# Attention scores of a head pair: one 128-row matmul with zero-padded queries, or two 64-row matmuls in the row halves of TensorE

## The chip, the cores and the metric

The kernel runs on one core of one Trainium2 chip. The metric is device time in microseconds (us) of one execution. Names used below: PE is TensorE's matmul stream, PEld its weight loads, DVE is VectorE, ACT is ScalarE, SP is the engine that issues many of the loads. A "profile" is one execution recorded by the hardware profiler; a "timed run" has only its time.

## The reference, cut to what matters

Attention over 8 batches of 8 heads with a window of 128 positions comes first. Its output goes through a mixture of 8 experts whose routing weights are normalised over all tokens.

```python
# q, k, v: (8, 8, 576, 64)
scores = scale * np.matmul(q, k.transpose(0, 1, 3, 2))
# ... bias by distance, mask (0 <= rel < 128), softmax
x = np.matmul(attn, v)                  # -> (4608, 512)
P = np.exp(x @ w_gate - max)            # ... eight rounds of row and column normalisation
for e in range(8):
    out += P[:, e:e+1] * (np.maximum(x @ w1[e], 0.0) @ w2[e])
```

## The kernel before

The head size is 64; the matmuls use up to 128 rows of TensorE (the trace lists them as 128*128, rows by columns). The kernel keeps two heads in one 128-row tile: head A in rows 0 to 63, head B in rows 64 to 127. To get two separate scores from one 128-row matmul, the queries are stored twice as wide, with zeros in the rows of the other head: `QZ[0:64, j, 0]` holds head A, `QZ[64:128, j, 1]` holds head B, the other two quarters are zero. The zeros are written once, at the start.

```python
KTs = [asb.tile([P, NPR, S], FP16, name=f"KT{i}") for i in range(2)]
QZs = [asb.tile([P, NPR, 2, S], FP16, name=f"QZ{i}") for i in range(2)]
...
def tr_unit(b, nm, j):                       # turns keys or queries of one head pair
    psT = aps.tile([P, RT, RP], FP16, ..., tag="pmm", bufs=4)
    ...                                      # 8 transposes on TensorE
    if nm == "k":
        nc.scalar.copy(out=KTs[b % 2][:, j, :]..., in_=psT...)
    else:
        QZ = QZs[b % 2]
        nc.vector.tensor_copy(
            out=QZ[0:64, j, 0, :].rearrange("p (c r i) -> p r c i", r=RT, i=HI),
            in_=psT[0:64].rearrange("p r (c i) -> p r c i", i=HI))
        nc.vector.tensor_copy(
            out=QZ[64:128, j, 1, :].rearrange("p (c r i) -> p r c i", r=RT, i=HI),
            in_=psT[64:128].rearrange("p r (c i) -> p r c i", i=HI))

def scores(b, kb, half):                     # key block kb, four heads; 80 calls in all
    ...                                      # nk keys (128 or 64), nq queries (256, 192 or 64)
    ps = aps.tile([P, 2, 2, 2 * P], FP32, ..., tag="psS")        # one buffer
    for jj in range(2):
        nc.tensor.matmul(
            out=ps[0:nk, jj, :, 0:nq],
            lhsT=KT[:, 2 * half + jj, k0 : k0 + nk],
            rhs=QZ[:, 2 * half + jj, :, k0 : k0 + nq])
    pt = asb.tile([P, 4, 2 * P], FP16, ..., tag=f"pt{half}", bufs=3)
    nc.scalar.activation(
        out=pt[0:nk, :, 0:nq],
        in_=ps[0:nk].rearrange("p a b q -> p (a b) q")[:, :, 0:nq],
        func=AF.Exp, scale=scale)
    ...
```

The output of attention is a matmul per head with 65 columns (`psN`). Its transposed copy (`psXT`), the turned keys and queries (`psT`), the routing scores (`psG`) and the two layers of expert 0 (`psh`, `psy`) share **one pool of four PSUM buffers**, the tag "pmm". So a matmul into the pool can be held up by whichever engine still reads the buffer that it is given (in the profile before, 0.38 us by ScalarE at 103.92 us, below):

```python
psT  = aps.tile([P, RT, RP], FP16, ..., tag="pmm", bufs=4)   # queries: read by VectorE
psXT = aps.tile([P, NDT, P], FP16, ..., tag="pmm", bufs=4)   # read by VectorE
psG  = aps.tile([P, E],     FP32, ..., tag="pmm", bufs=4)   # read by ScalarE
psh, psy: tag "pmm" too, 4                                   # read by ScalarE
```

Keys and queries of batch b + 2 are loaded while batch b is worked on. Expert 0 is interleaved with attention, so PE has something to do from about 50 us on. After attention the other experts run as a sequence of tasks; for each, the input block (`xl`) and a broadcast row of routing weights (`Pb`) are loaded three tasks ahead, and VectorE multiplies them before PE can use the result:

```python
def load_p(j):
    Pbs[j] = msb.tile([P, GT], FP32, name=f"Pb_{e}_{g}", tag="Pb", bufs=2)
    nc.sync.dma_start(out=Pbs[j], in_=PTr[e : e + 1, GT * g : ...].to_broadcast([P, GT]))

def load_next(h):
    if h + 3 < NT:
        load_x(h + 3, tasks[h + 3][1])
        load_p(h + 3)
```

The softmax here doesn't subtract the row's maximum and nothing guards it: scores larger than these inputs give would overflow.

## Time and profile before

| quantity | value | view |
|---|---|---|
| time, median of the first 6 runs | 1045.55 us (1045.15 to 1046.12) | timed runs |
| span of the profiled run | 1042.3 us | head of the page |
| attention ends (last routing-score matmuls) | 210.8 us | timeline |
| PE busy, 50 to 200 us | about 24 of each 25 us | table by stretches |
| VectorE busy there | about 18 of each 25 us | table by stretches |

The first lines of the page give busy time, share of the span and count of instructions:

```profile
PE 1004.1 (96%) x9163; PEld 817.6 (78%) x9163; DVE 841.7 (81%) x1318; ACT 647.9 (62%) x1176; POOL 233.6 (22%) x242
```

The table by stretches, of the kernel before. Columns: the stretch, then busy us and count of PE, PEld, DVE, ACT and POOL, as the first line has them.

```profile
core 0: us, PE busy (x) PEld busy (x) DVE busy (x) ACT busy (x) POOL busy (x), PEclk, DMA share, GB/s
...
50.00:75.00 25.00, 24.32 (x269) 14.38 (x266) 18.05 (x40) 17.59 (x30) 7.48 (x9) 1.00 0.83 97
```

PE is nearly full and VectorE has a quarter of its time free.

The timeline at 19 us, of the kernel before. Columns: start, length, engine, line, operation, output<-inputs, sizes, count, and in brackets the idle time before it and what ended it.

```profile
19.24 1.01 PE L237 MATMUL psS_1_0_228<-QZ_78,KT_76 128*128 128x512 f16 x2 [1.11 <-ACT pt_0_1_225 L245]
...
21.36 1.01 PE L237 MATMUL psS_1_1_234<-QZ_78,KT_76 128*128 128x512 f16 x2 [1.11 <-ACT pt_1_0_231 L245]
```

Here PE is not full: a half-block takes 21.36 - 19.24 = 2.12 us, of which PE idles 1.11 us until the exp has read the only scores buffer. And this is where the early stage ends, in the same view:

```profile
41.01 0.69 DVE L195 COPY kp_0_500<-kf_0_387 72x2048 f16<-72x2048 f16 x1
...
44.57 0.39 PE L325 MATMUL psXT_4_548<-ident,xsb_4_508 64*128 64x64 f16 x4
```

VectorE reorders the keys of batch 2 at 41.0 us, just after they have landed.

Last, what a change of the tile shape costs, at the end of attention in the same view. "128*128" is rows*columns of the array that the matmul uses.

```profile
205.84 0.29 PE L285 MATMUL psN_3_3124<-vsb_81,pt_3_0_3038 128*128 128x65 f16 x4
205.97 0.29 PE L285 MATMUL psN_3_3124<-vsb_81,pt_2_1_3001 128*128 128x65 f16 x4
...
207.41 0.32 PE L285 MATMUL psN_4_3146<-vsb_81,pt_3_0_3038 128*64 128x65 f16 x4 [1.02 <-DVE xsb_3_3123 L294]
207.65 0.31 PE L285 MATMUL psN_4_3146<-vsb_81,pt_4_0_3093 64*64 64x65 f16 x4
207.89 0.31 PE L285 MATMUL psN_4_3146<-vsb_81,pt_3_1_3066 128*64 128x65 f16 x4
```

Groups of four equal matmuls of one shape (`psN_3`) start 0.13 us apart. When the shape alternates between 128*64 and 64*64 (`psN_4`), they start 0.24 us apart.

### The profile page before, as it was taken

To read this page: it belongs to the slowest core of one execution; us is meant where nothing else is said; L and a number is where in the kernel's file an instruction comes from. 1 tells how busy PE (TensorE), PEld (TensorE's weight loads), DVE (VectorE), ACT (ScalarE), POOL (GpSimd) and SP (SyncE) were. 2 spreads that over 40 slices of the span, in tenths; PEclk is the share of its full clock that TensorE was granted. 3 is DMA by queue.
4 is the path that set the end of the run, shared out by engine and by line. 5 is a ranking of instruction groups with operands and counts; after the bars stand their busy time and mean duration, and the time that the engine had idled before them with its cause. 6 is when DMAs were issued, how large, how long until landed. Compare 5 with 4: busy or idle time off the path is not lost. (4 is left out here: it accounts for less than half of the span.)

```text
span 1042.3 us, 22521 instructions
## 1 busy us (share of the span) xinstructions
PE 1004.1 (96%) x9163; PEld 817.6 (78%) x9163; DVE 841.7 (81%) x1318; ACT 647.9 (62%) x1176; POOL 233.6 (22%) x242
## 2 busy tenths in 40 slices
PE   4999999999999999999999999999999999999996
PEld 2555555545888878888888888888888888888885
DVE  5777777576899988787788998888889988888875
ACT  3567666646899865665566656665665566655660
POOL 6332331020233321111112211111112112222234
PEclk9999999989999999999999999999999999999998
DMA  9977786184697795444436963444446646655546
GB/s 168 178 95 93 97 94 92 42 177 104 139 201 160 159 184 112 100 112 93 92 92 132 180 135 93 108 107 106 96 93 135 129 92 150 143 134 132 132 102 132
DMA packets 129609, 128.10 MB, mean 123 GB/s; under 512 B 49729, under 2 KB 107233, under 8 KB 129505
## 3 DMA queue, kind: packets, MB, share of 16 engines
q0 software_dynamic: 97376, 60.61, 43.6%
q1 hardware_dynamic: 31840, 65.79, 20.4%
q8 instruction: 71, 1.16, 0.4%
q14 instruction: 34, 0.27, 0.1%
q10 hardware_dynamic: 288, 0.26, 0.1%
HBM read 113.62 MB, written 16.66 MB: 125 GB/s over the span
## 5 line engine op out<-in xcount | busy, mean ns | idle before, releaser
L124 PEld LDWEIGHTS <-w1t_104 128*128 128x128 f16 x288 | 26.5, 100 | 29.2 <-issue 5.0
L654 PEld LDWEIGHTS <-w1t_3237 128*128 128x128 f16 x288 | 28.2, 98 | 5.2 <-issue 1.8
L654 PEld LDWEIGHTS <-w1t_3219 128*128 128x128 f16 x288 | 28.2, 98 | 4.8 <-issue 0.4
L654 PEld LDWEIGHTS <-w1t_8011 128*128 128x128 f16 x288 | 28.1, 98 | 4.4 <-issue 0.3
L654 PEld LDWEIGHTS <-w1t_7840 128*128 128x128 f16 x288 | 28.2, 98 | 4.0 <-issue 0.8
L654 PEld LDWEIGHTS <-w1t_5174 128*128 128x128 f16 x288 | 28.1, 98 | 3.8 <-issue 0.3
L654 PEld LDWEIGHTS <-w1t_10776 128*128 128x128 f16 x288 | 28.2, 98 | 3.6 <-issue 0.3
L654 PEld LDWEIGHTS <-w1t_3979 128*128 128x128 f16 x256 | 25.1, 98 | 2.9
L76 POOL DMA_DIRECT2D out_dram<-acc_lo x24 | 24.5, 1828 | 0.0
L184 POOL DMA_DIRECT2D vsb_81<-in_v_dram x20 | 17.8, 892 | 26.0 <-PE psN_4_905 L285 5.3
L184 POOL DMA_DIRECT2D vsb_80<-in_v_dram x20 | 18.3, 932 | 18.9 <-PE psN_4_1307 L285 5.7
L237 PEld LDWEIGHTS <-KT_76 128*128 128x128 f16 (+1 forms) x80 | 7.3, 106 | 13.1 <-issue 9.3
L506 POOL PARTITION_ALL_REDUCE ca_sb<-cs_sb x8 | 3.2, 396 | 64.0 <-DVE cs_sb L503 64.0
L310 PEld LDWEIGHTS <-xT 128*128 128x128 f16 x144 | 8.3, 100 | 8.4 <-DVE xT L334 1.6
L546 ACT ACTIVATE acc_lo<-acc_lo,Pe_sb 128x512 f32<-128x512 f32 (+1 forms) x24 | 14.8, 616 | 0.0
L237 PEld LDWEIGHTS <-KT_77 128*128 128x128 f16 (+1 forms) x80 | 7.1, 104 | 9.8 <-issue 5.5
L76 POOL DMA_DIRECT2D out_dram<-acc_hi x12 | 11.2, 2129 | 6.0 <-DVE acc_hi L770 6.0
L778 POOL DMA_DIRECT2D acc_lo<-st_1_0_3821 x1 | 1.2, 1242 | 36.3 <-ACT st_1_0_3821 L777 36.3
L654 PEld LDWEIGHTS <-ws_1_3535 128*128 128x128 f16 x72 | 6.9, 97 | 1.7 <-DVE xd_0_3543 L615 0.6
L654 PEld LDWEIGHTS <-ws_2_4301 128*128 128x128 f16 x72 | 7.0, 98 | 1.5 <-issue 0.7
L206 PE MATMUL psT_k_0_128<-ident,kp_0_124 72*128 72x72 f16 x8 | 0.7, 252 | 7.7 <-DVE kp_0_124 L195 7.7
L804 DVE TENSOR_TENSOR acc_lo<-acc_lo 128x512 f32<-128x512 f32 x12 | 7.7, 684 | 0.0
(4203 smaller groups left out, 3609.4 us busy)
## 6 DMA issues: line engine op xcount, KB each, us to landing
xTd<-xT SPq DMA_DIRECT2D x9, 512.0 KB
out_dram<-acc_lo SPq DMA_DIRECT2D x24, 128.0 KB
vsb_80<-in_v_dram POOLq DMA_DIRECT2D x16, 128.0 KB, 8.0
vsb_81<-in_v_dram POOLq DMA_DIRECT2D x16, 128.0 KB, 5.0
out_dram<-acc_lo SPq DMA_DIRECT2D x24, 64.0 KB
out_dram<-acc_lo POOLq DMA_DIRECT2D x24, 64.0 KB, 7.2
w1t_104<-in_moe_w_dram POOLq DMA_DIRECT2D x2, 512.0 KB, 10.4
w2t_117<-in_moe_w_dram POOLq DMA_DIRECT2D x1, 1024.0 KB, 15.1
```

The source lines that it names most:

```text
L76: eng.dma_start(out=out[t0 : t0 + HB, c0:c1].rearrange("(i r) d -> r i d", r=RT), in_=t[HB * c : HB * c + HB], **kw,)
L124: nc.tensor.matmul(out=psh, lhsT=w1t[:, dt, P * ft : P * ft + P], rhs=x[:, dt, :], start=(dt == 0), stop=(dt == NDT - 1),)
L184: nc.gpsimd.dma_start(out=vsb[0:nk, kb, :, 0:Dh], in_=v[b, :, k0 : k0 + nk, :].rearrange("h s d -> s h d"),)
L206: nc.tensor.matmul(out=psT[:, r, :], lhsT=tt[:, r, 2 * Dh * jj : 2 * Dh * jj + 2 * Dh], rhs=ident[0:RP, 0:RP], is_transpose=True, start=(r ...
L237: nc.tensor.matmul(out=ps[0:nk, jj, :, 0:nq], lhsT=KT[:, 2 * half + jj, k0 : k0 + nk], rhs=QZ[:, 2 * half + jj, :, k0 : k0 + nq],)
L310: nc.tensor.matmul(out=psG, lhsT=xT[:, dt, P * blk : P * blk + P], rhs=wg_sb[:, dt, :], start=(dt == 0), stop=(dt == NDT - 1),)
L506: nc.gpsimd.partition_all_reduce(ca_sb, cs_sb, P, bass_isa.ReduceOp.add)
L546: nc.scalar.mul(acc(blk)[:, c], acc(blk)[:, c], Pe_sb[:, 0, blk : blk + 1])
L654: nc.tensor.matmul(out=ps[:, f, :], lhsT=a[:, kt, f0 : f0 + P], rhs=b[:, kt, :], start=(m in (1, 5) and f == 0 and kt == 0), stop=(kt == 1 ...
L778: nc.gpsimd.dma_start(out=quad(self.g, rh, ch), in_=st, accum_op=ALU.add)
L804: tt(out=t, in0=t, in1=quad(g, 1, 1), op=ALU.add)
```

## The change

The intent: let each head of the pair use its own 64 rows of TensorE. The two row halves are to run at the same time, so that the two heads take the time of one, and no zeros are streamed. The queries need no padding, so each head pair is copied from PSUM by one VectorE instruction in place of two, and four memsets go. The layout of the scores in PSUM is swapped (head within the pair first), so that each row half writes its own half of the scores buffer, and the exp puts the order back.

```diff
-        QZs = [asb.tile([P, NPR, 2, S], FP16, name=f"QZ{i}") for i in range(2)]
+        QTs = [asb.tile([P, NPR, S], FP16, name=f"QT{i}") for i in range(2)]
@@ tr_unit
-                QZ = QZs[b % 2]
                 nc.vector.tensor_copy(
-                    out=QZ[0:64, j, 0, :].rearrange("p (c r i) -> p r c i", r=RT, i=HI),
-                    in_=psT[0:64].rearrange("p r (c i) -> p r c i", i=HI),
-                )
-                nc.vector.tensor_copy(
-                    out=QZ[64:128, j, 1, :].rearrange("p (c r i) -> p r c i", r=RT, i=HI),
-                    in_=psT[64:128].rearrange("p r (c i) -> p r c i", i=HI),
+                    out=QTs[b % 2][:, j, :].rearrange("p (c r i) -> p r c i", r=RT, i=HI),
+                    in_=psT.rearrange("p r (c i) -> p r c i", i=HI),
                 )
@@ scores
             for jj in range(2):
-                nc.tensor.matmul(
-                    out=ps[0:nk, jj, :, 0:nq],
-                    lhsT=KT[:, 2 * half + jj, k0 : k0 + nk],
-                    rhs=QZ[:, 2 * half + jj, :, k0 : k0 + nq],
-                )
+                for hh in range(2):
+                    rows = slice(Dh * hh, Dh * hh + Dh)
+                    nc.tensor.matmul(
+                        out=ps[0:nk, hh, jj, 0:nq],
+                        lhsT=KT[rows, 2 * half + jj, k0 : k0 + nk],
+                        rhs=QT[rows, 2 * half + jj, k0 : k0 + nq],
+                    )
...
-                out=pt[0:nk, :, 0:nq],
-                in_=ps[0:nk].rearrange("p a b q -> p (a b) q")[:, :, 0:nq],
+                out=pt[0:nk].rearrange("p (jj hh) q -> p hh jj q", hh=2)[:, :, :, 0:nq],
+                in_=ps[0:nk, :, :, 0:nq],
@@ start
-            for QZ in QZs:
-                nc.vector.memset(QZ[64:128, :, 0, :], 0.0)
-                nc.vector.memset(QZ[0:64, :, 1, :], 0.0)
```

More of the change, by code (lines that the diff above doesn't have):

```diff
@@ L233, in scores @@
             nq = min(2 * P, S - k0)
-            KT, QZ = KTs[b % 2], QZs[b % 2]
+            KT, QT = KTs[b % 2], QTs[b % 2]
             ps = aps.tile([P, 2, 2, 2 * P], FP32, name=f"psS_{b}_{kb}_{half}", tag="psS")
             for jj in range(2):
-                nc.tensor.matmul(
-                    out=ps[0:nk, jj, :, 0:nq],
-                    lhsT=KT[:, 2 * half + jj, k0 : k0 + nk],
-                    rhs=QZ[:, 2 * half + jj, :, k0 : k0 + nq],
-                )
+                for hh in range(2):
[5 more added lines that the diff above has]
+                    )
             pt = asb.tile(
```

## The prediction

> **What bounds the kernel now.** The change touches only attention, 0 to 211 us of 1042. In the table by stretches TensorE (PE) is busy about 24.2 of each 25 us from 50 to 200 us (VectorE 18, ScalarE 17), and PE's waits between 60 and 190 us sum to 5 us: the length of the PE stream binds. From 17 to 30 us the timeline shows another limit: half-block period 2.12 us, exp 1.02 us, then 1.1 us until the next scores are there (one scores buffer; granted clock half until 49 us). At 41.0 us VectorE reorders the keys of batch 2 just as they land (11.0 us after issue).
>
> **Removed.** Scores take 430 ns per call at full clock in key blocks 0-2 (two 512-column matmuls), 324 in block 3, 112 in block 4. Two concurrent 64-row matmuls halve that: 48 x 213 + 16 x 161 + 16 x 50 ns = 13.6 us at most. VectorE loses one of two 0.45 us query copies 32 times (14 us, but it has slack) and four 1.02 us memsets, which end before the first load lands: worth nothing.
>
> **Added.** 160 matmuls, and changes of PE's tile shape. [...]block 4 already uses 64-row and 64-column tiles, there starts are 121-124 ns apart where 32-33 is usual, 309 instead of 215 after a 512-column matmul; the next gap is 20-24 ns longer too. I take 94 + 24 ns going in, 94 + 10 coming out. In program order the shape changes 87 times in attention before, 201 after: 114 more.[...]
>
> A call at full clock then costs 94 + 24 + [...]214 + 104 = 463 ns against 430 (blocks 0-2), about 412 against 324 (block 3), some 26 ns less in block 4, where the switches exist. Some switches coincide with existing ones. Estimate for 50-205 us: 1.3 us lost[...].
>
> **Gained early.** First scores 0.5-1 us sooner (one query copy per pair); then 0.35 us per half-block while the chain exp, scores, exp rules at half clock[...]: 3 us by 30 us. The load landing at 40-41 us takes back part. I keep 2 us at 45 us. After attention everything only shifts.
>
> **Prediction.** 1045.55 - 2 + 1.3 = about 1045 us; 8 in 10 between 1041.5 and 1049.5. Faster by over 2%: 0.015; within: 0.95; slower by over 2%: 0.035.
>
> **What would show each step.**
> - [...]the second pair 107 ns after the first.
> - First start after a change of shape 94 ns later than the stream needs.
> - Half-block period at 19-28 us 1.75 instead of 2.12 us.
> - VectorE waiting for batch 2's keys near 40 us.
> - Last gate matmul within 3 us of 210.8 us.
> - VectorE busy 18 us less, the span unmoved by it.
>
> **What would make it wrong.** Row halves that do not overlap[...]; [...]the clock rising one step earlier or later than 49 us (its changes lie multiples of 3.4 us apart in this trace: 1.7 us either way), or falling again within attention.

Cut out of the text above is a term in the price of a call, for a later start of the second row half. With it the sum came to 463 ns; the terms that are left, 94 + 24 + 214 + 104, make 436 ns. The prices for blocks 3 and 4 seem to hold that term too, and the 1.3 us lost was worked out with it. A change of shape costs time; the price itself, 94 ns, is read from starts in the trace before (310 ns in place of 215 to the scores of block 4 at 109.48 us, 95 more).

Two of its statements, with their figures. That two 64-row matmuls run at once was an assumption; the trace after shows starts 3 ns apart at full clock. For the clock: in the trace before, 512-column matmuls start 427 ns apart up to 47.5 us and 215 ns apart from 48.3 us on. The recorded granted clock is 1.00 from 48.21 us, where its record begins (the views print 1.00 before that too, for want of a record), 0.50 from 208.63 and 1.00 again from 215.46 to 1034.66 us: stretches of 160.43, 6.83 and 819.20 us, or 47, 2 and 240 times 3.41 us. "Half clock" and "full clock" below mean these two.

## The result, and the profile after

| | before | after |
|---|---|---|
| median of all runs of the comparison | 1045.55 us (20 runs, 1042.37 to 1047.67) | 1044.61 us (10 runs, 1041.09 to 1046.48) |
| ratio | 1 | 0.9989, 95% interval 0.9978 to 1.0000 |
| profiled run | 1044.11 us, span 1042.3 | 1046.57 us, span 1044.7 |

Ratios here are the mean time of one kernel's runs over the mean of the other's of the same rounds, so they are not quite the ratio of the medians quoted. The verdict is "same": about 1 us faster. The profiled run of the kernel after was slower than all its timed runs, so the two spans stand the other way round; single profiles of one kernel here scatter by some 2 us. For that reason both kernels were profiled a second time (rep_before and rep_after below), and what is read from the profiles is read from stages, not from the span.

The page after, first lines and the lines by stretch and on the timeline that answer to those above:

```profile
PE 998.8 (96%) x9323; PEld 811.2 (78%) x9323; DVE 821.2 (79%) x1282; ACT 647.5 (62%) x1176; POOL 233.5 (22%) x242
```

```profile
50.00:75.00 25.00, 24.57 (x294) 13.95 (x291) 16.46 (x37) 17.97 (x32) 7.49 (x9) 1.00 0.90 102
```

```profile
18.83 0.61 PE L234 MATMUL psS_1_0_224<-QT_78,KT_76 64*128 64x256 f16 x4 [1.11 <-ACT pt_0_1_221 L242]
...
20.55 0.61 PE L234 MATMUL psS_1_1_232<-QT_78,KT_76 64*128 64x256 f16 x4 [1.11 <-ACT pt_1_0_229 L242]
...
42.89 0.69 DVE L195 COPY kp_0_510<-kf_0_393 72x2048 f16<-72x2048 f16 x1 [4.81 <-DMA kf_0_393<-in_k_dram]
...
45.07 0.39 PE L322 MATMUL psXT_4_562<-ident,xsb_4_520 64*128 64x64 f16 x4 [4.20 <-DVE xsb_4_520 L291]
```

Three readings. VectorE is busy 841.7 - 821.2 = 20.5 us less. A half-block of the early stage takes 20.55 - 18.83 = 1.72 us where it took 2.12. And at 42.9 us VectorE has waited 4.81 us for the keys of batch 2, where it had work before: whatever was gained by then is waited away, and the next matmuls start 0.50 us later than before (45.07 against 44.57). The load was issued at 29.67 us, 0.29 us sooner than before, and took 13.2 us where it had taken 11.0 (13.9 against 10.2 in the second pair); why it took longer is not shown.

Now the whole span, cut at four marks of the timeline: the second `psh` group of expert 0 (attention interleaved with expert 0 from there on), the last `psy` of it (`psy_23`), and the last routing-score matmuls, with which attention ends.

| stage, us | before | rep_before | after | rep_after |
|---|---|---|---|---|
| start to the second psh group | 48.30 | 48.05 | 48.63 | 48.18 |
| from there to psy_23 | 155.35 | 155.70 | 151.66 | 152.24 |
| to the last routing scores | 7.22 | 7.23 | 7.18 | 7.18 |
| all after attention | 831.43 | 833.62 | 837.24 | 838.03 |
| span | 1042.3 | 1044.6 | 1044.7 | 1045.6 |

So the middle of attention is 3.5 to 3.7 us shorter, in both pairs, and the part after attention, which the change does not touch, is 4.4 to 5.8 us longer. The lines at the end of attention, before and then after:

```profile
210.77 0.27 PE L310 MATMUL psG_3191<-wg_sb,xT 128*128 128x8 f16 x4 [0.39 <-DVE xT L334]
```

```profile
207.36 0.27 PE L307 MATMUL psG_3315<-wg_sb,xT 128*128 128x8 f16 x4 [0.39 <-DVE xT L331]
```

**The middle of attention: what PE's stream gained.** This is one scores call after, at full clock (granted clock 1.00 from 48.6 to 205.5 us), from the timeline, with the one before it on PE:

```profile
98.40 1.03 PE L124 MATMUL psh_2_0_1484<-xT,w1t_100 128*128 128x512 f16 x4
...
99.37 0.39 PE L234 MATMUL psS_2_1_1493<-QT_79,KT_77 64*128 64x256 f16 x4
...
99.69 0.30 PE L282 MATMUL psN_1_1501<-vsb_81,pt_0_0_1316 128*128 128x65 f16 x4
...
101.07 0.42 PE L206 MATMUL psT_q_1_1528<-ident,qp_0_1372 72*128 72x72 f16 x8
...
101.86 0.45 DVE L220 COPY QT_78<-psT_q_1_1528 128x576 f16<-128x576 f16 x1
...
102.36 0.59 PE L124 MATMUL psh_2_2_1569<-xT,w1t_100 128*128 128x512 f16 x2
```

and the same work before:

```profile
100.39 0.59 PE L237 MATMUL psS_2_1_1444<-QZ_79,KT_77 128*128 128x512 f16 x2
...
100.83 0.29 PE L285 MATMUL psN_1_1450<-vsb_81,pt_0_0_1274 128*128 128x65 f16 x4
...
102.20 0.42 PE L206 MATMUL psT_q_1_1477<-ident,qp_0_1328 72*128 72x72 f16 x8
...
102.98 0.44 DVE L221 COPY QZ_78<-psT_q_1_1477 64x576 f16<-64x576 f16 x1
...
103.44 0.46 DVE L225 COPY QZ_78<-psT_q_1_1477 64x576 f16<-64x576 f16 x1
103.69 0.17 ACT L317 ACTIVATE P_sb<-psG_1495 128x8 f32<-128x8 f32 x1
...
103.92 0.59 PE L124 MATMUL psh_2_2_1517<-xT,w1t_104 128*128 128x512 f16 x2 [0.38 <-ACT P_sb L317]
```

Matmuls with 512 columns start 0.215 us apart here, so the four of `psh_2_0` after have streamed by 98.40 + 0.86 = 99.26; the scores start at 99.37, some 0.1 us late, and the next group starts at 99.69. The call has cost 99.69 - 99.26 = 0.43 us (0.420 us by the unrounded starts). Before, it cost 100.83 - 100.39 = 0.44 us (0.432 us unrounded). The two halves together stream in half the time (by estimate twice 107 ns, half of the 215 ns of a 512-column matmul, in place of twice 215), and the two changes of shape take it back. The single starts in the trace show it: 96 ns beyond the stream going into the scores, then 3, 116, 3 ns between the four matmuls, and 202 ns from the last one to the next group, that is its 107 ns and 95 more.

Over the whole stretch I summed PE's start-to-start gaps. "Scores" is what the scores take, with what they add to the gap in front of them and behind them; "other waits" is all that the other gaps have beyond the streaming time.

| stretch from the second psh group to psy_23, us | before | after |
|---|---|---|
| scores with their changes of shape | 30.04 | 28.17 |
| other changes of shape | 3.44 | 3.42 |
| other waits | 5.95 | 4.16 |

Half of the gain is the scores (1.87 us), the other half is waits that have nothing to do with scores (1.79 us). The lines at 102 to 104 us show one of them: `psh_2_2` waits for a buffer of the shared pool. Before, two readers end shortly before it starts at 103.92: the second query copy (103.44 + 0.46 = 103.90), which reads `psT_q_1`, and ScalarE's `P_sb` (103.69 + 0.17 = 103.86), which reads `psG`. The bracket names `P_sb`, and pe_only, an experiment below that keeps both copies, shows that this is right. The same place there:

```profile
101.53 0.46 DVE L225 COPY QZ<-psT_q 64x576 f16<-64x576 f16 x1
...
101.73 0.17 ACT L319 ACTIVATE P_sb<-psG 128x8 f32<-128x8 f32 x1
...
101.95 1.02 PE L124 MATMUL psh<-xT,w1t 128*128 128x512 f16 x4 [0.28 <-ACT P_sb L319]
```

The matmul starts at 101.95, before the second copy ends at 101.99, and 0.05 us after `P_sb` ends, as in the kernel before. After, with one copy that ends at 101.86 + 0.45 = 102.31, `psh_2_2` starts at 102.36, with no idle time listed, and before `P_sb` begins (102.52). So it no longer waits for the same buffer. The programs agree: `psh_2_2` is given the buffer of `psG` in before and pe_only, and that of `psT_q_1` in after and dve_only. The second copy thus costs time at one remove: while it reads, the buffer of `psT_q_1` is not free (until 103.90), and the buffer given in its place is not free sooner. Waits of about 0.55 us stand six times in the profile before; five are for `P_sb`, one is for the second query copy itself. After, three of 0.44 us are left, all for `P_sb`, and the others are 0.07 us or less.

**After attention.** The view of waits of PE from 215 us on. Columns: engine, tile and line that waited, what it waited for, us in total, times, longest. Before:

```profile
PE lb_0_1_5245 L654 <- DVE lc_0_1_5270 L693: 1.3, 1, 1.3
PE lb_0_1_8271 L654 <- DVE lc_0_1_8301 L693: 0.6, 1, 0.6
```

and after:

```profile
PE lb_1_1_5624 L648 <- DVE lc_1_1_5655 L687: 1.5, 1, 1.5
PE lb_0_1_5369 L648 <- DVE lc_0_1_5394 L687: 1.4, 1, 1.4
PE lb_0_1_8395 L648 <- DVE lc_0_1_8425 L687: 1.3, 1, 1.3
PE lb_7_1_5023 L648 <- DVE lc_7_1_5052 L687: 1.0, 1, 1.0
```

All idle times of PE over 0.05 us from 215 us on sum to 3.46 us before (5.28 in rep_before) and 7.44 us after (8.64 in rep_after); the expectations below quote an earlier count, which is 0.1 to 0.4 us higher. VectorE itself was late at those places because a routing-weight row had not landed. One pair, on the timeline, before:

```profile
335.58 0.43 SPq L590 DMA_DIRECT2D Pb_8_4801<-PTd  x1
...
342.02 1.22 DVE L597 TENSOR_TENSOR xl_4799<-xl_4799,Pb_8_4801 128x1024 f16<-128x1024 f16 x1
...
387.03 1.22 DVE L597 TENSOR_TENSOR xl_5406<-xl_5406,Pb_1_5408 128x1024 f16<-128x1024 f16 x1
```

and after:

```profile
333.25 0.53 SPq L584 DMA_DIRECT2D Pb_8_4925<-PTd  x1
...
340.85 1.23 DVE L591 TENSOR_TENSOR xl_4923<-xl_4923,Pb_8_4925 128x1024 f16<-128x1024 f16 x1 [1.06 <-DMA Pb_8_4925<-PTd]
...
387.69 1.23 DVE L591 TENSOR_TENSOR xl_5530<-xl_5530,Pb_1_5532 128x1024 f16<-128x1024 f16 x1 [1.78 <-DMA Pb_1_5532<-PTd]
```

The load has about 6.5 us from issue to use, with nothing to spare: before, it was just enough here, after, it was 1.06 us too late, and 1.78 us too late four loads on.

### The profile page after: what moved, and what is told of

The parts are those of the page before. It is cut to its first block, busy times and chain, and to the rows that moved or that the text cites. A ratio compares the mean times of both kernels' runs of the same rounds, so it can differ in the third digit from the quotient of the medians. Undisturbed runs are those within 1.5% of the kernel's fastest.

```text
span 1044.7 us, 22776 instructions
## 1 busy us (share of the span) xinstructions
PE 998.8 (96%) x9323; PEld 811.2 (78%) x9323; DVE 821.2 (79%) x1282; ACT 647.5 (62%) x1176; POOL 233.5 (22%) x242
## 5 line engine op out<-in xcount | busy, mean ns | idle before, releaser
L234 PEld LDWEIGHTS <-KT_76 64*128 64x128 f16 (+1 forms) x160 | 6.0, 100 | 14.7 <-issue 12.7
L234 PEld LDWEIGHTS <-KT_77 64*128 64x128 f16 (+1 forms) x160 | 5.3, 97 | 13.5 <-issue 12.6
L307 PEld LDWEIGHTS <-xT 128*128 128x128 f16 x144 | 6.1, 98 | 7.4 <-issue 5.1
```

The costliest lines, as they stand in the source:

```text
L234: nc.tensor.matmul(out=ps[0:nk, hh, jj, 0:nq], lhsT=KT[rows, 2 * half + jj, k0 : k0 + nk], rhs=QT[rows, 2 * half + jj, k0 : k0 + nq],)
L307: nc.tensor.matmul(out=psG, lhsT=xT[:, dt, P * blk : P * blk + P], rhs=wg_sb[:, dt, :], start=(dt == 0), stop=(dt == NDT - 1),)
```

## The experiments

Twelve kernels ran, in three groups; the kernels of one group ran on the same chip. The first group asks whether the gain of the middle of attention comes from PE or from VectorE, and whether the loss after attention is systematic. Its runs of the kernel before had the median 1046.25 us.

### rep_before and rep_after: the two kernels once more

Edit: none, identical copies.

> The kernel before, profiled again on this chip. Last gate matmul within 1 us of 210.8 us unless the first loads land at other times. Waits of TensorE after 215 us: theory N says they differ from the 3.6 us of the first profile by 1 us or more; rival S says 3.6 us again. Ratio 1.000 within 0.001.

> The changed kernel once more, for its scatter. In the first profile its attention ended 3.2 us earlier than before (last gate matmul 207.6 against 210.8 us), and 4.4 us were lost again after attention, in waits of TensorE for VectorE that waited for the loads of the routing weights. Theory N (noise): these landings vary from run to run whatever the kernel; then this profile loses another amount after attention, by 1 us or more, while attention ends at 206.5 to 209 us. Rival S (systematic: the shift of phase costs it): the same loss of about 4 us in the same places. Ratio 0.9975 to 1.0005.

Measured: rep_before 1046.28 us, ratio 1.0000 (0.9987 to 1.0014); rep_after 1045.34 us, ratio 0.9992 (0.9979 to 1.0005). The stages are in the table above. The loss after attention came again (833.62 to 838.03, 4.4 us), at the same places. Matched matmul by matmul from the end of attention, PE falls behind by 0.6 and 0.9 us near 307 us (first and second pair), by 1.1 and 1.0 us near 345 us and by 1.6 and 1.2 us near 391 us, where it is 3.9 us behind in both pairs. So it is systematic, though its size scatters: one profile of the kernel before had 2.2 us more of it than the other. In the timed runs the loss must be smaller than in these two profiles. An estimate from the shift at the end of attention (3.4 us) and the medians (0.9 us) is 2.5 us.

### pe_only: two row halves, padded queries kept

```diff
-                nc.tensor.matmul(
-                    out=ps[0:nk, jj, :, 0:nq],
-                    lhsT=KT[:, 2 * half + jj, k0 : k0 + nk],
-                    rhs=QZ[:, 2 * half + jj, :, k0 : k0 + nq],
-                )
+                for hh in range(2):
+                    rows = slice(Dh * hh, Dh * hh + Dh)
+                    nc.tensor.matmul(
+                        out=ps[0:nk, hh, jj, 0:nq],
+                        lhsT=KT[rows, 2 * half + jj, k0 : k0 + nk],
+                        rhs=QZ[rows, 2 * half + jj, hh, k0 : k0 + nq],
+                    )
```

(and the exp with its order, as in the change; both query copies and the memsets stay)

> TensorE part of the change alone: 64-row pairs of matmuls, but the two query copies and the memsets of before are kept. Theory P: from 50 to 200 us the gain of 3.6 us comes from the scores on TensorE (call 421 against 434-510 ns in blocks 0-2, 275 against 326 in block 4, 368 against 327 in block 3); then this kernel gains 3 to 4 us in this stretch too. Rival V: it comes from VectorE's saved copies; then it gains under 1 us there. Total within 1.5 us of the changed kernel under P.

### dve_only: one query copy, 128-row matmuls

The kernel after, with one 128-row matmul per head pair that reads the unpadded queries twice. The scores are wrong (they mix the two heads), the work per instruction is that of before. The comparison with the reference cannot be relied on to catch such an error.

```diff
-                for hh in range(2):
-                    ...
-                        rhs=QT[rows, 2 * half + jj, k0 : k0 + nq],
+                nc.tensor.matmul(
+                    out=ps[0:nk, jj, :, 0:nq],
+                    lhsT=KT[:, 2 * half + jj, k0 : k0 + nk],
+                    rhs=QT[:, 2 * half + jj, k0 : k0 + nq].unsqueeze(1).to_broadcast([P, 2, nq]),
+                )
```

> VectorE part alone: one query copy, no memsets, and 128-row matmuls that read the unpadded queries twice. The scores are wrong on purpose (both heads of a pair added), the work and its times are those of before. Theory P: from 50 to 200 us it gains under 1.5 us against before (a few short waits for the query copy vanish). Rival V: 3 to 4 us. Start: first exp up to 1 us sooner under both.

Measured, both: pe_only 1045.00 us, ratio 0.9990 (0.9977 to 1.0003); dve_only 1044.59 us, ratio 0.9984 (0.9972 to 0.9996). The account of PE's gaps:

| us | before | pe_only | dve_only | after |
|---|---|---|---|---|
| scores with their changes of shape | 30.04 | 28.17 | 30.06 | 28.17 |
| other waits | 5.95 | 6.74 | 4.36 | 4.16 |
| end of attention | 210.87 | 207.38 | 208.27 | 207.47 |
| waits of PE after attention | 3.46 | 6.14 | 5.03 | 7.44 |

The two parts are separate: the matmuls take 1.87 us from the scores and nothing from the waits, VectorE's single copy takes 1.6 us from the waits and nothing from the scores. (The end of attention of pe_only is as early as that of after because its stretch began 2.5 us sooner, at 46.10 us; part of that time ran at half clock, and part of its waits are from there.) The length of the stretch says the same. As an estimate, take off half of the time in it at half clock (until 47.2 to 49.3 us in these six profiles; in before and after the record of the granted clock, 1.00, begins at 48.21 and 48.56 us): the stretch then lasts 155.4 us in both profiles of before, 153.7 in pe_only, 153.4 in dve_only and 151.7 in both profiles of after. The parts gain 1.7 and 2.0 us, together the 3.7 us of the change. Both theories that gave the whole gain to one engine fell. None of the three variants is worth over 2 us in time, and each has more waits after attention than the first profile of before (not more than rep_before, 5.28 us, in the case of dve_only).

### early_p_before and early_p_after: the routing weights loaded one task sooner

This takes away the cause of the late loss in both kernels, if it is that the loads have no slack.

```diff
         def load_next(h):
             if h + 3 < NT:
                 load_x(h + 3, tasks[h + 3][1])
-                load_p(h + 3)
+            if h + 4 < NT:
+                load_p(h + 4)
 
+        load_p(2)
         load_next(-1)
```

> The kernel before, with each load of routing weights issued one task earlier (same two buffers). In the profiles so far TensorE waits 3.6 and 5.4 us after attention in the kernel before, 7.8 and 9.1 us in the changed one, and the extra lies in the same three places in both profiles of it (near 308, 345 and 392 us), where VectorE waits for a routing-weight load. Theory L: these loads have no slack, and the changed kernel meets more late ones. Then here the waits at 368 and 600 us shrink, and this kernel gains 1 to 2 us on before (ratio 0.998 to 0.9995). Rival: the waits come from elsewhere, ratio 1.000.

> The changed kernel with the same earlier loads. Theory L: its late waits fall by 3 to 5 us, the gain of 3.4 us in attention stays, and it runs 4 to 6 us under the kernel before (ratio 0.9945 to 0.997) and 2.5 to 4 us under the twin of before with the early loads. Rival: the loss after attention is something else, then the ratio stays at 0.999.

Measured (before: 1045.33 us in this group): early_p_before 1044.63 us, ratio 0.9990 (0.9976 to 1.0003); early_p_after 1039.30 us (1038.02 to 1041.26), ratio 0.9939 (0.9926 to 0.9952). In the kernel before, the earlier load is worth about 1 us or nothing. In the kernel after it is worth some 5 us, and with it on both sides the change gains 1044.63 - 1039.30 = 5.3 us where it gained 0.9 us without. The stages of the two profiles:

| us | early_p_before | early_p_after |
|---|---|---|
| end of attention | 211.41 | 206.88 |
| all after attention | 831.44 | 832.56 |

Attention ends 4.5 us sooner and 1.1 us of it is lost later. So the gain did exist, and what hid it was late loads after attention. The 5.3 us are more than the 2.5 to 4 us expected, and the two profiled runs differ by 3.4 us only (that of early_p_after was the slowest of its five), so some 2 us of the 5.3 are in no profile. Part of what profiles differ by is the clock: at the end of attention it fell to half for 6.8 us in early_p_before and for 3.4 us in early_p_after, which by estimate is worth up to 1.7 us (half of the 3.4 us between them). Of the two waits that the earlier load was to shrink in the kernel before, the one near 369 us (1.27 us, 1.36 in rep_before) went; the one near 600 us stayed (1.46 us). early_p_after computes the right result and beats both kernels: it is the best version found. Some waits are left in it:

```profile
PE lb L648 <- DVE lc L687: 2.4, 5, 1.7
```

### serial: the four matmuls of a call in another order

The two upper row halves first, then the two lower ones; if only neighbours in program order overlapped, the concurrency would be mostly lost.

```diff
-            for jj in range(2):
-                for hh in range(2):
+            for hh in range(2):
+                for jj in range(2):
                     rows = slice(Dh * hh, Dh * hh + Dh)
```

> The changed kernel with the order of the four matmuls of a score call changed: both of the upper row half, then both of the lower. Same work, same number of changes of shape. Theory C (two row halves run at the same time only where they follow one another in the stream): start gaps of about 107, 3, 107 ns instead of 3, 116, 3 ns at blocks 0-2, so a call is about 105 ns longer, 75 in block 3, 25 in block 4; 66 calls at full clock make +5 us by the end of attention. Rival: concurrency plays no part (the records are modelled), then no change.

Measured: 1047.14 us, ratio 1.0009 (0.9995 to 1.0024). The timeline of a call:

```profile
99.10 0.40 PE L234 MATMUL psS<-QT,KT 64*128 64x256 f16 x4
99.43 0.68 PE L282 MATMUL psN<-vsb,pt 128*128 128x65 f16 x16
```

The call takes 99.43 - 99.10 = 0.33 us from its first matmul to the next group, against 0.32 us in the kernel after (99.69 - 99.37), the built program has the order upper, upper, lower, lower, and the recorded starts of the four are 0, 6, 120 and 126 ns: two pairs, as in the other order. In strict program order and with one stream at a time in each row half, the four would need three times 107 ns (upper; upper with lower; lower) and the 95 ns of the change of shape, 0.42 us. That did not happen. If the recorded starts are those of the streams, a later matmul of the other row half went ahead of an earlier one. The trace does not say which row half a record belongs to, so this rests on the length of the call. The run therefore does not take the concurrency away, and as a test of what it is worth it failed: the scores take 6.97 us within the calls, against 6.75 us.

### twice: double the changes of shape

One tiny 128-row matmul in the middle of each call adds two changes of shape per call, 160 in all. The place it writes is overwritten by the next pair, so the result stays right.

```diff
+                if jj == 0:
+                    nc.tensor.matmul(
+                        out=ps[0:nk, 0, 1, 0:8],
+                        lhsT=KT[:, 2 * half, k0 : k0 + nk],
+                        rhs=QT[:, 2 * half, k0 : k0 + 8],
+                    )
```

> The changed kernel with two more changes of tile shape in each score call: between its two pairs stands one 128-row matmul of 8 columns, whose output is overwritten by the next pair (results stay right). It doubles the suspected cost. Theory D (each change [...]costs about 95 ns between starts plus about 10 to 24 ns[...]): +200 to 230 ns for each of about 66 calls at full clock, +13 to 15 us at the last gate matmul, total 1057 to 1061 us. Rival: the gaps of 95 ns are hidden elsewhere, then under +4 us.

Measured: 1056.40 us, ratio 1.0103 (1.0089 to 1.0118).

```profile
100.68 0.28 PE L234 MATMUL psS<-QT,KT 64*128 64x256 f16 x2
100.89 0.18 PE L240 MATMUL psS<-QT,KT 128*128 128x8 f16 x1
101.01 0.28 PE L234 MATMUL psS<-QT,KT 64*128 64x256 f16 x2
```

The two 256-column halves stream 0.107 us; the tiny matmul starts 0.21 us after them, 0.1 us late, and the second pair 0.12 us after that. The stretch in the middle grows from 151.66 to 165.41 us; against a mean of four profiles with the scores of after (152.4: after, rep_after, serial, early_p_after) that is about 13 us for the 65 calls in it, 200 ns per call. So the price of two changes, some 190 ns, and 10 to 20 ns of the tiny matmul are on the critical path in full. The total came out slightly below what was expected.

### filler: the kernel after, with its later instructions moved

In most profiles of the first two groups, the late routing-weight loads had something in common: a packet of another queue close to their issue (dve_only is an exception, see the table). The page lists it:

```profile
q8 instruction: 71, 1.16, 0.4%
```

for the kernel before, and

```profile
q8 instruction: 73, 1.20, 0.5%
```

for the kernel after. I take these to be PE's own instructions: packets of 16,384 bytes, about 14 us apart, and their count goes with PE's: 18,349 instructions and 71 packets before, 18,668 and 73 after, one for some 256 to 258 instructions (18,349 / 71 = 258, 18,668 / 73 = 256). The change adds 319 instructions in attention, so all later packets come at other points of the program. For two of the loads, the time of the packet after the issue of the load, and how long VectorE then waited:

| kernel | packet at load 8 (near 340 us) | wait | packet at load 12 (near 387 us) | wait |
|---|---|---|---|---|
| before | +6.0 us | 0 | +7.8 us | 0 |
| rep_before | +6.1 | 0 | +7.0 | 0 |
| after | +0.7 | 1.06 us | +4.9 | 1.78 us |
| rep_after | +0.6 | 0.91 | +3.9 | 1.31 |
| pe_only | +0.6 | 0.13 | +5.3 | 0.67 |
| dve_only | +7.4 | 0.45 | +8.1 | 0 |
| serial | +2.6 | 0.42 | +4.0 | 1.40 |
| twice | +7.8 | 0 | none | 0 |

The filler adds 96 tiny matmuls, 192 more PE instructions, during attention, where PE waits anyway (4.20 us at 45.07 us in the kernel after), so that all later packets should move to near where they were in the kernel before (319 + 192 = 511 instructions are about two packets, by the ratio above). If the packets are the cause, the waits go, although PE has more work.

```diff
+                if i == 6:
+                    psF = aps.tile([P, E], FP32, name="psF", tag="pmm", bufs=4)
+                    for _ in range(96):
+                        nc.tensor.matmul(
+                            out=psF, lhsT=xT[:, 0, 0:P], rhs=wg_sb[:, 0, :]
+                        )
```

> The changed kernel with 96 idle matmuls of 8 columns (192 TensorE instructions), put where TensorE waits some 4 us for the keys of batch 2 near 41 us; their output is never read. The loads of TensorE's instructions, 16 KB each, appear in the trace some 14 us apart; the changed kernel has 319 instructions more than before, so they fall elsewhere: inside the routing-weight loads issued near 334 and 381 us, which then land 0.7 to 1.8 us too late, and outside of them in the kernel before and in the run with doubled switches. With 511 instructions more than before[...] they fall as before. Theory F (instruction loads delay these two loads): waits at 345 and 392 us vanish, the span after the last gate matmul falls from 837-838 to 832-835 us, total 1041 to 1043.5 us. Rival (the phase of something else): as the changed kernel, 837 us and 1044.6 us.

Measured (before: 1044.65 us in this group): 1043.44 us, ratio 0.9984 (0.9971 to 0.9998). The packets came at +7.3 us (load 8) and +6.5 us (load 12), and both waits were 0. All after attention took 833.90 us, against 837.24 and 838.03 of the kernel after (and 831.43 and 833.62 of before); PE's waits there summed to 4.15 us, against 7.44 and 8.64.

So with the packets moved both loads came in time, as expected, in one profile. The time itself moved by little: the ratio 0.9984 is only 0.0005 below that of the kernel after (0.9989), well inside the intervals. Four things stay open. Why a packet should delay the load is not shown. In dve_only load 8 was 0.45 us late with its packet at +7.4 us, where it did not hurt in filler and twice. A third load, near 306 us, speaks against the packets: it was 1.5 to 1.9 us late in after, rep_after and pe_only with no packet beside it, and only 0.6 and 0.8 us late in before and rep_before, with a packet about 1 us after its issue (1.3 us late here, with one at +1.6 us). And pe_only with its packet at +0.6 us waited only 0.13 us, so the packet is not all that counts.

### pe_early and dve_early: the two parts, with early loads

pe_only and dve_only, each with the early routing-weight loads. If the late loads hid the gain of each part, it should show now.

> TensorE part alone, with the early routing-weight loads, so that late loads do not blur the total. The two earlier early-load kernels ran at 1044.63 (before) and 1039.3 us (changed). Accounts of TensorE's starts from 48 to 204 us: the scores give 1.87 us (30.0 to 28.2 us) in every kernel with row halves; the other 1.6 us are waits that vanish with the second query copy. Theory H (half and half): 1041.5 to 1043.5 us here. If the row halves were all of it: 1039.5.

> VectorE part alone (scores wrong on purpose), with the early routing-weight loads. Theory H: 1041 to 1043.5 us, and its gain and that of the TensorE part add up to about the 5.3 us between the two early-load kernels within 1.5 us. If the VectorE part were all: 1039.5.

Measured: pe_early 1042.75 us, ratio 0.9974 (0.9958 to 0.9990); dve_early 1040.67 us, ratio 0.9962 (0.9948 to 0.9975), slightly lower than expected. Against early_p_before (0.9990, of the second group; so this compares ratios across two groups) PE's part is worth 0.16% or 1.7 us, VectorE's part 0.28% or 2.9 us, both 0.51% or 5.3 us: about the sum. The intervals overlap, so which part is the larger is not settled; that VectorE's part is worth something is, since the interval of dve_early lies below that of early_p_before (0.9976 to 1.0003). That of pe_early (up to 0.9990) does not: what PE's part is worth in time is not clear of the noise, and is read from the profiles.

### paired_early: both halves' scores in one go, fewer changes of shape

An attempt at a better version: if a call's cost is mostly the changes of shape, doing both calls of a key block in one go needs half of them. That takes a second scores buffer in PSUM, and with it two of the four buffers of the shared pool.

```diff
-            ps = aps.tile([P, 2, 2, 2 * P], FP32, name=f"psS_{b}_{kb}_{half}", tag="psS")
+            ps = aps.tile([P, 2, 2, 2 * P], FP32, name=f"psS_{b}_{kb}_{half}", tag=f"psS{half}")
...
-            tag="pmm", bufs=4        (all five users)
+            tag="pmm", bufs=2
...
-                pt0, mask0 = scores(b, kb, 0)
+                if i > 0:
+                    pt0, mask0 = scores(b, kb, 0)
+                    pt1, mask1 = scores(b, kb, 1)
```

> The changed kernel with early routing-weight loads, and both score calls of a block next to each other, so that 132 instead of 201 changes of tile shape are left in attention. It needs a second scores buffer[...], taken from the shared matmul buffers (2 instead of 4). Theory D says that 69 changes of about 100 ns are worth 6 to 7 us of TensorE stream; waits for the fewer shared buffers cost an unknown part or more than that. Faster than 1039.3 us if they cost under 6 us; I expect 1034 to 1046 us.

Measured: 1063.59 us, ratio 1.0179 (1.0162 to 1.0196), outside all that was expected. The scores did shrink, from 28.17 to 21.98 us, as hoped. The other waits of the stretch grew from 4.16 to 30.04 us; some 2.7 us of that, as an estimate (half of the time at half clock), are the clock, which was at half until 49.5 us and for 3.4 us again near 75 us. The view of PE's waits from 50 to 210 us, its first lines:

```profile
PE psT_k L206 <- DVE xT L331: 4.3, 9, 0.5
PE psXT L322 <- DVE QT L220: 3.5, 4, 1.1
```

Users of the shared pool now wait for the readers of two buffers. Six microseconds were bought with more than 20. It also shows, from the other side, how much the pool's readers matter. Whether the pairing pays with all four buffers was not tried.

## Why the prediction was right or wrong

The number was right: 1045 us predicted, 1044.61 us measured, "within 2%". The sum behind it was not; its errors went in opposite directions and cancelled.

- **"half-block period at 19-28 us 1.75 instead of 2.12 us"**: right, 1.72 us.
- **"VectorE waiting for batch 2's keys near 40 us"**: right, a wait of 4.81 us at 42.9 us. But **"I keep 2 us at 45 us"** was wrong: nothing is kept, the next matmuls start 0.50 us later than before. In all 14 profiles these keys landed between 39.9 and 42.9 us, however fast attention ran. The prediction treated the load as something that takes back a part; it took back everything.
- **"94 + 24 ns going in, 94 + 10 coming out"**: the 94 was right, both ways (95 to 97 ns in, 93 to 95 ns out). The rest of the call was priced too high. The second row half starts 3 ns after the first, where the term that is cut above had it later. Beyond the stream of 214 ns and twice 94 ns, the prediction added 61 ns in all (24, 10 and that term), and the trace has 18 ns. A call of key blocks 1 and 2 costs 421 ns, not 463, against 434 before.
- **"Estimate for 50-205 us: 1.3 us lost"**: that a call would gain next to nothing is right (0.42 us and 0.43 us in the lines above: the two changes of shape, 96 and 95 ns, take back what the pairs save). The size is off: the scores gained 1.87 us. Besides the 42 ns per call, key block 0 cost 510 ns before and not 430, because changes of shape stood there already, and block 4 gained 51 ns a call where 26 had been said.
- **"VectorE loses one of two 0.45 us query copies 32 times (14 us, but it has slack) ... worth nothing"**: wrong, for the copies. They are worth 1.6 us of the middle of attention (dve_only) and, with early loads, about 2.9 us of the total. VectorE does have slack on average (before, busy 18.05 of the 25 us from 50 to 75 us); but while the second copy reads, it keeps a buffer of the shared pool, and a matmul that follows waits up to 0.55 us: in one of the three places that the change cleared for that copy, in two for another buffer that it was given and that ScalarE was still reading. So most of this wait did not show under VectorE's name.
- **"Last gate within 3 us of 210.8 us"**: missed: it came at 207.4 us, 3.4 us sooner. That is the sum of the points above: 0.3 us lost early, 3.7 us gained in the middle, where 2 us gained and 1.3 us lost had been said.
- **"VectorE busy 18 us less, the span unmoved by it"**: 20.5 us less; the span is moved by it, when nothing later takes it back.
- **"After attention everything only shifts"**: wrong, and this is the error that cancelled the others. The part after attention became 4.4 to 5.8 us longer in the profiles (about 2.5 us in the timed runs, by the estimate above). Loads of routing weights that had been just in time came late: early_p_after gave the loads more time, and the gain of attention came out, 5.3 us. Instruction packets (q8) now fell beside two of these loads, and in filler, which moved the packets, the two waits were gone; but a load was late in dve_only without a packet beside it, so why they came late is only in part known.

Put as a sum: predicted -2 + 1.3 + 0. In the two profile pairs: about 0 early, -3.6 in the middle, +5 later. In the timed runs about -1.

Of the 5.8 and 4.4 us lost after attention, PE's idle times explain 4.0 and 3.4 us. Up to its last matmul PE is 4.9 and 4.3 us behind, the rest of the loss (0.9 and 0.1 us) comes after it.

## What to carry to other kernels

Before splitting a matmul into concurrent row halves, set the streams saved against the two changes of shape around them: here each call saved 0.21 us and paid 0.19 us. Grouping the calls in paired_early brought the scores from 28.17 to 21.98 us, but it cost buffers, and other waits grew from 4.16 to 30.04 us. Before calling an engine's work free because the engine has slack, look at which buffer it holds while it works, who needs that buffer next, and which buffer they get in its place. And when a gain of one stage does not arrive at the end, look behind that stage for loads that were just in time: issuing one kind of load a task earlier turned 1 us into 5.
